# A delta-rule attention and gated layer on one core: the state product as one 64-column tile, the solve on pairs of batch elements, results moved by ScalarE, and another written order

## The chip, the cores and the metric

The kernel runs on one core of one Trainium2 chip. The metric is the device time of one execution in microseconds, lower is better. TensorE (PE in the profile) multiplies matrices, VectorE (DVE), ScalarE (ACT) and GpSimd (POOL) work on elements, SyncE (SP) issues the transfers. All data are 32-bit floats.

## The reference

Two parts, the second fed by the first. For each of 4 batch elements (B) and 8 heads (H), over 768 tokens of 48 numbers:

```python
k_n = k / (norm(k) + 1e-6)
for t in range(S):                       # state is 48 x 48, zero at first
    y[t] = q[t] @ state
    v_old = k_n[t] @ state
    state = state + beta[t] * outer(k_n[t], v[t] - v_old)
```

Then, with x the 3072 x 384 matrix of all y (a row per batch element and token, all heads side by side):

```python
h = x @ w_in                             # 384 -> 2048
out = (h * cos(h)) @ w_out               # 2048 -> 384
```

## The kernel before

**Units.** The 768 tokens are cut into 24 units n of C = 32 tokens. In a unit the 4 batch elements lie in the four quarters of the 128 partitions, and the 8 heads are written as h = 2j + par, with j of 4 pairs and par of 2. The recurrence of a unit is solved in closed form: with the Gram matrix of its keys, the inverse of a 32 x 32 triangular matrix for each batch element and head gives all corrected values at once. Two units form a pair m, which shares one inverse.

**Steps of a unit**, as the tasks are called in the function that writes the program:

- `k`, `q`, `v` load; `square`, `sum`, `norms`, `scale`, `weigh` make the norms and the weights by beta. The root in `norms` is on GpSimd (L467).
- `turn`, `turn_out` transpose keys and queries: for n < 8 on TensorE with two copies by ScalarE (L525), later by `blocks` loads and one VectorE transpose (L531).
- `gram` (L546) multiplies keys with keys and queries; `gram_keys`, `gram_queries` scale the two results; `gram_put`, `gram_get` carry the Gram matrices through DRAM into the layout of the inverse.
- `inv` (L656, L663) is the inverse of pair m on GpSimd, in seven pieces of columns (pair 0 on VectorE, by halves); `put`, `get` carry it through DRAM back into `zt`.
- `state` (L713) multiplies keys and queries with the state of the units before. It runs over a (keys or queries), j, b and par: 64 matmuls, each with 32 weight columns and 48 moving columns, into the quarter of its batch element.
- `right` (L728, VectorE) subtracts the product with the keys, read from PSUM, from the values; `solve` (L776) multiplies with the inverse: 32 matmuls of 32 x 32 weights, one for each head and batch element; `solve_out` (L786) weighs the result.
- `update` (L799), `update_out` (L807) add to the state: 16 matmuls of 64 x 64 weights and 96 moving columns.
- `within` (L816) adds the part of the unit's own tokens to the product with the queries, in the same PSUM tile `p_kq`; `within_out` (L827, ScalarE, one copy of 128 x 384) takes it out; `features`, `features_out` (L835, L843) transpose it for the second part.

So the chain from unit to unit is state, right, solve, solve_out, update, update_out.

**The second part** works on one pair's 256 tokens p at a time: `hidden` (L856) or `layer` (L975) for the first product, `turns`, `rest`, `cos`, `gate` for h cos(h) on ScalarE and VectorE, `out` (L1001, L1058) for the second product. From p = 2 (first product) and p = 1 (second) on a scheme of seven products in place of eight is used, with sums by VectorE. The weights come as pairs of 32-bit words and are narrowed once at the start: `weights` (load), `split` (ScalarE), `shift` (VectorE), `add` (GpSimd, L438), 28 tiles, of which 0 to 11 are `w_in`.

**The order** is written out by hand. Each step is a task with an engine and the tasks it depends on; a list of numbers, `Order.LINE`, gives the place of every task in the program. Each engine takes its own tasks strictly in this order, and so does the transfer queue of SP. The costs that stand beside the tasks are not used when the program is written.

**Buffers.** `p_kq` and the tile for the smaller products (`two`) have one PSUM buffer each, the first product of the second part has three. `zt` has two buffers.

Of the kernel before, what the change touches and what calls it, by code (L numbers as in the profile page):

```python
# [53 lines left out]
0 1767 1 2 14 10 11 12 3 7 4 37 5 42 15 72 6 38 13 39 16 43 73 40 1768 1771 17 44 19 96 75 1769 97  # L54
79 18 1770 45 46 1775 80 76 48 47 77 20 99 104 1772 100 78 101 1779 1773 105 81 102 1774 49 82 106
50 83 84 1776 107 1783 108 9 131 51 22 52 109 1787 53 1780 36 1784 54 155 1781 55 56 132 1777 1788
41 1778 1791 111 1789 134 1782 110 1785 21 1790 138 8 1786 135 1795 23 139 136 186 818 1792 24
1793 112 25 137 1799 1796 26 57 27 113 1797 28 1803 74 29 30 1794 156 32 31 114 1807 140 33 210
141 142 34 58 115 35 1811 1808 98 189 59 1804 60 190 1798 679 61 1815 1800 116 103 133 1809 1805
1819 62 241 680 1812 1810 63 681 64 117 65 1820 66 1823 68 67 187 69 1821 159 682 118 265 1801 684  # L60
160 1816 1827 161 1817 685 86 162 1824 163 686 70 1822 119 87 71 143 1813 193 1802 243 1825 1818
689 1831 1828 683 164 1826 194 1829 85 687 1830 690 688 1806 719 1835 691 731 165 1814 732 1832
244 88 191 166 822 694 692 1833 1839 157 1836 89 1834 1837 90 695 92 1838 696 1843 699 693 697 167
91 93 1840 698 94 1841 700 704 1847 168 1844 701 211 192 95 702 709 703 1845 1848 1851 1842 120
733 705 714 1846 1849 710 158 1850 711 195 1855 169 712 121 196 197 198 706 720 713 707 122 715
1859 708 1856 170 716 747 1857 717 123 1863 1860 296 752 124 1852 245 718 748 749 125 753 1853
1858 127 750 126 757 1864 1854 1867 188 754 128 171 751 755 735 129 1865 758 762 130 759 1871 1868
320 756 760 1861 1866 214 763 736 767 1862 215 737 761 172 764 1869 765 772 1875 248 1872 766 768
1873 216 247 769 1874 145 246 1876 1870 777 217 773 1877 219 298 269 739 770 1878 740 721 774 173
771 775 743 778 220 299 722 212 779 744 780 745 782 249 723 221 300 724 776 788 174 725 783 268  # L70
784 222 741 785 726 218 819 823 824 144 223 825 727 820 821 302 146 786 728 224 781 303 213 147
729 734 175 148 787 225 149 789 151 791 351 790 150 152 738 153 793 792 176 154 226 794 177 270
242 178 796 179 795 227 180 798 182 375 181 799 183 301 184 800 185 228 826 827 250 828 742 730
829 324 251 252 801 831 830 353 253 833 842 271 832 843 266 200 834 844 835 272 229 845 802 274
836 354 804 273 355 201 323 837 839 838 806 846 797 275 807 276 847 850 199 808 267 848 840 809
230 851 849 852 810 841 277 803 854 202 853 858 855 304 860 859 278 856 203 357 862 857 204 863
805 206 890 358 279 811 207 861 205 873 864 812 406 231 874 865 875 814 232 280 233 866 234 813
868 867 876 297 235 746 281 869 237 236 815 430 877 878 208 870 325 209 238 879 816 282 239 881
871 880 240 378 882 921 872 920 889 922 885 321 283 892 883 886 408 305 884 379 895 255 887 306
409 923 307 308 891 356 925 410 888 896 926 893 284 326 817 894 898 327 924 329 328 927 936 900  # L80
897 929 322 901 254 930 928 902 411 330 331 931 256 285 933 903 937 932 938 904 940 939 906 941
332 257 942 908 934 944 943 258 333 909 935 905 910 948 945 949 259 946 261 950 334 461 947 952
911 984 954 953 951 262 260 956 359 912 335 957 899 958 413 955 286 907 967 959 960 412 287 336
968 962 961 380 913 969 352 963 288 914 971 964 289 337 970 290 972 292 485 291 973 916 975 263
976 917 338 974 977 965 293 918 264 978 376 987 294 983 295 966 1014 915 1015 979 433 1017 1016
980 463 981 1019 339 1018 434 360 982 1030 310 361 1020 985 1021 1031 363 362 1023 1032 464 986
1024 1022 309 465 1033 381 989 1025 382 383 384 990 988 1026 992 311 1034 340 1027 994 991 919 414
312 1038 385 995 386 467 1039 1035 996 1040 313 1036 1028 997 993 387 1037 314 1029 316 516 315
1042 998 317 1043 388 1046 466 1044 318 341 319 1041 1047 1078 1000 342 468 377 389 1048 1045 407
1050 1049 1001 1052 1051 1002 343 1053 390 1054 344 1056 1055 431 345 1057 347 346 1003 348 540  # L90
391 435 1065 1061 1004 1066 349 1067 1005 1058 1062 999 1068 1006 392 488 1069 1007 1063 1070 1059
1064 1071 1008 350 393 1009 1010 1072 489 1081 1109 1060 1011 1108 1073 1110 1111 1012 518 1074
519 1113 1075 1077 1112 520 432 1124 1080 1013 1114 394 1125 415 1076 1126 365 416 1083 417 418
1115 469 1084 366 523 1116 1086 1082 1127 1117 1079 364 436 1118 1088 1119 437 438 439 1089 1087
1120 1090 1128 367 1129 1121 368 1130 440 441 1085 369 1132 395 1131 371 1133 1122 372 1091 571
1134 1092 1123 442 370 1136 1094 1135 1137 1140 1172 396 522 1141 443 1096 1138 1095 1142 397 1093
462 1139 1144 1143 444 398 1145 1146 1155 1148 1147 399 1097 1149 486 1156 1150 445 1157 1098 1151
1159 400 1099 402 595 401 1100 521 446 373 1158 1152 374 490 403 404 1160 1101 544 1161 1153 447
405 1162 1163 1102 470 1154 1103 420 1164 1167 471 573 1203 1168 473 448 1165 1104 472 1202 1169
491 1204 1170 1105 1166 492 1205 493 494 1106 421 1207 1206 1209 524 1218 449 1171 1208 1219 1174  # L100
1175 495 1210 1211 1177 1173 1213 574 1212 419 1220 1178 1214 575 1221 1180 1222 1107 496 543 1223
1215 1179 497 1224 1176 1216 1226 1225 578 1227 1234 1182 498 1228 1217 422 450 1183 1230 423 1181
577 1184 1229 499 424 1185 1231 426 626 1186 427 1232 1235 1188 1187 425 500 1236 1233 1238 1237
1190 1240 1239 1249 451 1241 501 1250 1242 452 1251 1244 545 517 1243 453 1245 1191 1252 1253 502
454 1192 455 1193 1254 457 650 456 1194 1255 503 1256 428 1246 429 487 458 1189 459 1195 460 576
541 1257 1247 1196 1258 1197 598 525 628 1296 475 1259 1248 1198 526 504 1261 527 599 1260 1199
1269 546 1200 1297 528 547 548 1265 1262 1266 549 1263 1268 1267 1264 1299 1271 505 579 1298 629
1301 1201 1303 1300 1302 630 550 1272 1312 1304 474 1270 1305 476 1307 1313 1306 633 551 1274 1308
1314 631 552 1309 632 1315 1276 477 1320 1277 478 553 1273 1278 1321 479 1275 1322 1279 481 1316
1323 1310 554 482 1317 480 1318 1280 1311 1319 1282 1324 555 506 1325 1328 507 1283 1330 572 1329  # L110
1284 1326 600 1332 556 1327 508 1333 1331 1334 509 1343 1336 1281 596 510 1344 512 557 511 1345
654 1285 1337 1335 542 483 1338 484 653 1286 1339 558 1346 1347 1340 513 1348 514 1287 1351 1341
1360 1349 1352 515 1288 1353 1390 1289 1354 580 1290 559 1350 530 1291 581 1342 1292 583 582 1355
1293 1356 1363 601 1357 1294 1391 602 1393 1358 1392 604 634 1395 1394 560 1359 1396 1406 1362
1407 605 606 1397 531 1365 1295 1408 1399 1398 529 1361 1366 1400 603 1409 1401 1368 1402 607 1410
1403 1370 1364 1367 532 1414 1411 608 1404 1412 1415 533 1416 1371 1417 1372 1413 609 1405 1422
597 1418 1424 1423 1419 1373 534 1420 1425 610 536 535 1374 537 1437 1376 1438 1375 561 1439 611
1440 1426 1378 1428 562 1427 1377 1379 627 655 563 1429 612 1380 564 1430 1369 1454 565 1431 651
567 566 1432 613 538 1433 1434 568 1421 539 1441 1381 569 1445 1382 1442 1446 1383 1443 1447 1435
1384 570 1444 1448 614 1485 1385 1436 1487 1486 1449 635 1450 585 636 1451 1488 638 1386 1484 1500  # L120
1387 637 584 1457 656 1388 1489 657 658 659 1453 586 1490 1501 1456 1452 1502 1491 1459 1503 587
1455 1493 1492 660 588 1495 1494 615 1460 1496 1458 1389 1462 1504 661 1505 589 662 591 1506 590
1497 1507 1464 1498 1508 663 1509 1516 1499 1510 1465 1463 1512 1511 1517 1466 664 1518 1467 1513
1514 1520 1519 1468 1515 1521 665 592 1548 1522 1531 1470 1523 1532 1524 1472 1533 1469 1526 1525
# [53 lines left out]
def kernel(  # L178
# [502 lines left out]
    def get(n):  # L681
# [13 lines left out]
        for b in range(B):  # L695
            queue("get", n).dma_start(out=zts[n][quarter(b)], in_=z_dr[b])
# [845 lines left out]
```

## Time and profile before

| | us |
|---|---|
| median of 3 runs | 670.01 |
| lowest and highest | 668.9, 674.3 |
| span of the profiled execution | 670.2 |
| busy in it: TensorE | 616.5 |
| VectorE, ScalarE, GpSimd | 466.5, 242.4, 347.1 |
| TensorE's mean granted clock | 0.995 |

The profiled execution has no time of its own beside its span, from its first instruction to its last; the span is within 0.1% of the median of the runs. Busy times overlap across engines, so the largest share does not by itself say what sets the end. The state product's records sum to 33.5 us over 23 units, the solve's to 19.7 us over 22, the update's to 21.8 us over 23.

### The profile page before, as it was taken

The numbers are of one execution on the slowest core, as the hardware profiler recorded it, in microseconds if no ns is written. First come the engines' busy times: TensorE is split into PE (matmuls) and PEld (weight loads), VectorE is DVE, ScalarE is ACT, GpSimd is POOL, SyncE is SP. The second block draws the span as 40 slices with busy tenths as digits, with TensorE's granted clock in tenths as the row PEclk, the third lists the DMA queues.
The fourth block names the chain that finished last, engine by engine and source line by source line (L and its number), as shares of the span: only waits on it lengthen the run. The fifth ranks groups of instructions, "written<-read, shape, count | busy, mean of one in ns | idle before, by whom it ended". The sixth has DMA issues, their size and how long they took to land.

```text
span 670.2 us, 27723 instructions
## 1 busy us (share of the span) xinstructions
PE 616.5 (92%) x12120; PEld 580.5 (87%) x12120; DVE 466.5 (70%) x892; ACT 242.4 (36%) x416; POOL 347.1 (52%) x734
## 2 busy tenths in 40 slices
PE   4326789999999999999999999999999999999996
PEld 3225779976889999999999999999999999999996
DVE  6872698897577777787767767777776666656662
ACT  3441565650223433334334332333323333332420
POOL 4268778988728658238458484385383382000000
PEclk9999899999899999999999999999999999999999
DMA  8776594464364523544443624623312302000000
GB/s 179 183 177 156 130 228 124 105 110 66 53 103 68 85 54 57 89 88 70 70 83 55 108 35 73 106 39 53 69 27 39 68 2 40 20 2 24 1 25 24
DMA packets 215645, 51.80 MB, mean 77 GB/s; under 512 B 207076, under 2 KB 210420, under 8 KB 215524
## 3 DMA queue, kind: packets, MB, share of 16 engines
q1 hardware_dynamic: 212516, 49.16, 38.0%
q8 instruction: 95, 1.56, 1.0%
q10 hardware_dynamic: 2752, 0.43, 0.4%
q0 software_dynamic: 256, 0.44, 0.2%
q14 instruction: 26, 0.21, 0.1%
HBM read 39.24 MB, written 10.75 MB: 75 GB/s over the span
## 4 chain that ended last, share of the span: by engine, by line
PE 79%; DMA 7%; SPq 4%; POOL 4%; DVE 2%; issue 2%; ACT 0%; ACTq 0%; DVEq 0%; POOLq 0%
PE p_h L975 28%; PE p_out L1058 27%; PE p_h L856 5%; PE p_kq L713 4%; PE p_out L1001 3%; PE p_u L776 3%; PE p_s L799 3%; PE p_kq L816 2%; PE p_g L546 2%; POOL z L663 2%; DMA pairs<-in_moe_w_in_dram 2%; POOL part L656 2%; PE p_o L1058 2%; DMA qp<-in_q_dram 1%; SPq L310 1%
## 5 line engine op out<-in xcount | busy, mean ns | idle before, releaser
L656 POOL TENSOR_TENSOR part<-z,gb 128x126 f32<-128x126 f32 (+22 forms) x341 | 134.6, 395 | 116.1 <-DMA gb<-g_dr 75.0
L663 POOL TENSOR_TENSOR z<-z,part 128x126 f32<-128x126 f32 (+22 forms) x341 | 138.7, 407 | 26.7
L975 PE MATMUL p_h<-x_ffn,w_in 128*128 128x128 f32 x1120 | 143.0, 277 | 0.0
L975 PEld LDWEIGHTS p_h<-x_ffn,w_in 128*128 128x128 f32 x1120 | 134.2, 192 | 1.5
L1058 PE MATMUL p_out<-w_out,g_ffn 128*128 128x192 f32 x672 | 121.8, 330 | 2.0 <-issue 2.0
L1058 PEld LDWEIGHTS p_out<-w_out,g_ffn 128*128 128x128 f32 x672 | 108.7, 191 | 3.3 <-issue 2.1
L896 ACT ACTIVATE turns<-p_h,quarter_turn 128x512 int32<-128x512 f32 x96 | 65.8, 688 | 105.6 <-DVE p_h L994 72.1
L912 ACT ACTIVATE turns<-turns,halfpi 128x512 f32<-128x512 f32 x96 | 68.7, 721 | 64.3 <-DVE turns L903 63.7
L1058 PE MATMUL p_out<-w_sum,g_ffn 128*128 128x192 f32 x496 | 88.7, 329 | 0.0
L903 DVE SCALAR_TENSOR_TENSOR turns<-p_h,turns 128x512 f32<-128x512 f32 x96 | 65.3, 683 | 22.0 <-ACT turns L896 22.0
L1058 PEld LDWEIGHTS p_out<-w_sum,g_ffn 128*128 128x128 f32 x496 | 79.7, 190 | 0.8
L991 ACT COPY g_ffn<-p_h 128x512 f32<-128x512 f32 x60 | 35.0, 584 | 108.8 <-PE p_h L975 108.7
L1074 DVE TENSOR_TENSOR g_ffn<-g_ffn 128x512 f32<-128x512 f32 x88 | 62.3, 715 | 10.0 <-PE p_out L1058 8.9
L915 DVE TENSOR_TENSOR g_ffn<-turns,p_h 128x512 f32<-128x512 f32 x96 | 64.6, 677 | 6.6 <-ACT turns L912 6.5
L994 DVE TENSOR_TENSOR p_h<-g_ffn,p_h 128x512 f32<-128x512 f32 x60 | 41.5, 692 | 30.5 <-PE p_h L975 23.7
L467 POOL TENSOR_TENSOR knrm<-ksum,halves 128x16 f32<-128x16 f32 (+1 forms) x14 | 36.2, 2590 | 41.5 <-DVE ksum L455 41.5
L1108 DVE SCALAR_TENSOR_TENSOR o<-p_out,o 128x192 f32<-128x192 f32 x74 | 25.2, 353 | 35.4 <-PE p_out L1058 33.9
L856 PE MATMUL p_h<-x_ffn,w_in 128*128 128x128 f32 x384 | 47.3, 282 | 2.3 <-POOL part L656 2.1
L856 PEld LDWEIGHTS p_h<-x_ffn,w_in 128*128 128x128 f32 x384 | 45.8, 197 | 3.3 <-issue 2.2
L975 PE MATMUL p_h<-x_sum,in_sum 128*128 128x128 f32 x320 | 41.6, 277 | 0.0
L786 DVE TENSOR_TENSOR u<-p_u,bz 128x384 f32<-128x384 f32 x48 | 24.4, 550 | 21.9 <-PE p_u L776 21.8
L975 PEld LDWEIGHTS p_h<-x_sum,in_sum 128*128 128x128 f32 x320 | 38.7, 192 | 0.5
(110 smaller groups left out, 767.2 us busy)
## 6 DMA issues: line engine op xcount, KB each, us to landing
pairs<-in_moe_w_in_dram SPq DMA_DIRECT2D x12, 512.0 KB
pairs<-in_moe_w_out_dram SPq DMA_DIRECT2D x16, 384.0 KB
gb<-g_dr SPq DMA_DIRECT2D x22, 256.0 KB
vp<-in_v_dram SPq DMA_DIRECT2D x96, 48.0 KB
out_dram<-o SPq DMA_DIRECT2D x23, 192.0 KB
kp<-in_k_dram SPq DMA_DIRECT2D x128, 24.0 KB
z_dr<-z SPq DMA_DIRECT2D x11, 256.0 KB
zt<-z_dr SPq DMA_DIRECT2D x88, 32.0 KB
```

What stands on the lines that cost most here:

```text
L467: nc.gpsimd.tensor_tensor(out=scales[m][2][:, part], in0=sums[m, part.start][:, 0:n], in1=halves[:, 0:n], op=ALU.pow,)
L656: eng.tensor_tensor(out=part, in0=z[:, 0:rows, j, None].to_broadcast(shape), in1=a[:, j, None, j + 1 :].to_broadcast(shape), op=ALU.mult,)
L663: eng.tensor_tensor(out=behind, in0=behind, in1=part, op=ALU.subtract)
L856: nc.tensor.matmul(p_h[:, i], w_in[:, t, (4 * k + i) * 128 : (4 * k + i + 1) * 128], xts[p][:, t, unit * 128 : (unit + 1) * 128], start=(t ...
L896: nc.scalar.activation(turns[p, f], hidden_of(p, f), AF.Identity, bias=quarter_turn, scale=TURN)
L903: nc.vector.scalar_tensor_tensor(out=r, in0=hidden_of(p, f), scalar=TURN, in1=t, op0=ALU.mult, op1=ALU.subtract,)
L912: nc.scalar.activation(r, r, AF.Sin, bias=halfpi, scale=2.0 * math.pi)
L915: nc.vector.tensor_tensor(out=place(p, f), in0=step_of(rests.pop((p, f)), f), in1=step_of(hidden_of(p, f), f), op=ALU.mult,)
L975: nc.tensor.matmul(p_h[:, e], in_sum[:, odd_tile, 4 * s + e] if a == "s" else w_in[:, a, f * 128 : (f + 1) * 128], x_sums[p][:, unit] if b ...
L994: nc.vector.tensor_tensor(out=block(p, s, 0, 1) if i == 3 else p_h, in0=block(p, s, *one), in1=p_h, op=ALU.add,)
L1058: nc.tensor.matmul(p_o, left(p, part, a)[:, e % 4], right(e, b), start=(e == 0), stop=(e == FT // 2 - 1), skip_group_check=True,)
L1074: nc.vector.tensor_tensor(out=left(p, s, to), in0=left(p, s, one), in1=left(p, s, two), op=op)
```

## The change

1. **State product.** Transposed keys and queries of one batch element and head pair lie side by side: `kq_t` changes from (side, batch and pair, token) to (batch and pair, side, token). In odd batch elements the queries come first. One matmul takes all 64 columns as weights: 32 matmuls for 64. For batch elements 2i and 2i + 1 the result is a half of the partitions; the product with the keys of batch element b stands in quarter b, as before, that with its queries in quarter b xor 1.
2. **Moves.** `turn_out` for n < 8 is four ScalarE copies in place of two, `turn_blocks` three VectorE transposes in place of one, of as many elements in all. The loads of `blocks` write another place, with as many transfers of the same size.
3. **Old values.** A new task `old` (L735 of the new kernel) copies the product with the keys from PSUM into `rhs` by ScalarE, four copies of 32 partitions; `right` then subtracts SBUF from SBUF.
4. **Solve.** Two lasting tiles `zt_pairs`, zeroed once by GpSimd, hold the inverses of batch elements 2i and 2i + 1 as diagonal blocks of 64 x 64. For n > 1 the solve is 16 matmuls for 32. For n < 8 both parities write the half they read from, from n = 8 on the odd parity writes the other half. `get(n)` now depends on `solve(n - 2)`.
5. **Output.** `within` writes into quarter b xor 1, and `within_out` is four copies of 32 partitions.
6. `part` and `fold` share one lasting tile.

```diff
     def turn_out(n):
         kq_t = turned(n)
         p_t = p_ts.pop(n)
         for a in range(2):
-            nc.scalar.copy(
-                kq_t[:, a].rearrange("p (b j) t -> p j b t", b=B),
-                p_t[:, a].rearrange("p j (b t) -> p j b t", b=B),
-            )
+            for x in range(2):
+                nc.scalar.copy(
+                    sides(kq_t, x)[:, a ^ x].rearrange("p b j t -> p j b t"),
+                    p_t[:, a].rearrange("p j (b x t) -> p x j b t", x=2, t=C)[:, x],
+                )
...
-                        kq_t[rows48(par), 0, b * NP + j],
-                        kq_t[rows48(par), :, b * NP + j],
+                        kq_t[rows48(par), b * NP + j, b % 2],
+                        kq_t[rows48(par), b * NP + j, :: 1 - b % 2 * 2],
...
-        zts[n] = work.tile([128, H, C], FP, name="zt")
+        zts[n] = zt_pairs[n % 2]
...
-            queue("get", n).dma_start(out=zts[n][quarter(b)], in_=z_dr[b])
+            queue("get", n).dma_start(
+                out=zts[n][quarter(b), :, b % 2], in_=z_dr[b]
+            )
...
-        for a in range(2):
+        for x in range(2):
             for j in range(NP):
-                for b in range(B):
+                for i in range(2):
                     for par in range(2):
                         nc.tensor.matmul(
-                            p_kq[quarter(b), par, a, j],
-                            kq_t[rows48(par), a, b * NP + j],
-                            st[rows48(par), b // 2, j, b % 2],
-                            start=(j == 0 and a == 0),
-                            stop=(a == 0),
+                            p_kq[half(i), par, x, j],
+                            kq_t[rows48(par), (2 * i + x) * NP + j].rearrange("p s t -> p (s t)"),
+                            st[rows48(par), i, j, x],
+                            start=(j == 0 and x == 0),
+                            stop=True,
                             skip_group_check=True,
                         )
+
+    def old_values(n):
+        rhs = rhss[n] = work.tile([128, H, D], FP, name="rhs", bufs=1)
+        for b in range(B):
+            nc.scalar.copy(by_parity(rhs[quarter(b)]), p_kqs[n][quarter(b), :, b % 2])
...
-        rhs = rhss[n] = work.tile([128, H, D], FP, name="rhs", bufs=1)
-        nc.vector.tensor_tensor(
-            out=by_parity(rhs),
-            in0=by_parity(vt),
-            in1=p_kqs[n][:, :, 0],
-            op=ALU.subtract,
-        )
+        nc.vector.tensor_tensor(out=rhss[n], in0=vt, in1=rhss[n], op=ALU.subtract)
...
-                for b in range(B):
-                    h = 2 * j + par
-                    nc.tensor.matmul(
-                        p_u[home(n, b, par), par, j], zt[quarter(b), h], rhs[quarter(b), h]
-                    )
+                h = 2 * j + par
...
+                for i in range(2):
+                    to = half(1 - i if n >= PLAIN_TURNS and par else i)
+                    nc.tensor.matmul(p_u[to, par, j], zt[half(i), h], rhs[half(i), h])
...
-        nc.scalar.copy(by_parity(y), p_kqs.pop(n)[:, :, 1])
+        p_kq = p_kqs.pop(n)
+        for b in range(B):
+            nc.scalar.copy(by_parity(y[quarter(b)]), p_kq[quarter(b ^ 1), :, b % 2])
```

7. **The order.** `Order.LINE` is new as a whole. Read back into tasks, these are the stretches that the text below speaks of. (`inv1,0` is the first piece of inverse 1; numbers after a task are its unit, tile or pair.)

```
GpSimd before: norms0,0 norms0,1 add0 norms1,0 norms1,1 add1 add2 add3 add5 add4 norms2 inv1,0 inv1,1
               add6 inv1,2 inv1,3 add7 inv1,4 add10 inv1,5 inv1,6 add13 add8 add12 add14 add15 add9 add11
GpSimd after:  norms0,0 norms0,1 norms1,0 norms1,1 add1 add2 inv1,0 add0 norms2 inv1,1 inv1,2 add5 add3
               inv1,3 add4 inv1,4 add7 add6 inv1,5 inv1,6 add10 add8 add12 add9 add11 add13 add15 add14
SP before, from gram_put3:  gram_put3 weights5 v1 k5 put0 q4 weights6 gram_get1 get0 ... v4 weights13 k8
               weights14 q6 k9 weights15 put1 gram_put4 weights16 gram_put5 get2
SP after:      gram_put3 v0 weights5 k4 gram_get1 v1 put0 k5 weights6 get0 ... k8 weights12 q5 weights13
               v3 weights14 put1 q6 weights15 gram_put5 get2
SP before, after solve5:  k13 store0,1 blocks11,1 gram_put8 v9 put3 gram_put9 blocks11,0 gram_get4 get6
SP after, after solve5:   blocks11,1 blocks10,0 store0,1 v8 gram_put9 put3 gram_put8 gram_get4 get6
TensorE before: state1 solve_half1 hidden0,0 between1 solve1 update1 within1 turn5 hidden0,2 gram5 state2
TensorE after:  state1 features0 hidden0,0 solve_half1 hidden0,2 between1 solve1 update1 turn5 within1 gram5 state2
TensorE after, unit 5: within4 out1,0,1 state5 features4 out1,1,0 solve5 ... within5 out1,2,0 features5
```

In the new order TensorE has long stretches of other work between state product and solve in the even units from 4 on, and little in the odd ones: `features` and a half `out` in unit 5, `layer` 5 and 6 in unit 7, `layer` 3 and 4 and a half `out` in unit 9, two halves of `out` in unit 13, and two to six such pieces in the others.

## The prediction

> **What bounds the kernel now.** I read the page first: the shares, the slices and the chain.
>
> ```profile
> PE 616.5 (92%) x12120; PEld 580.5 (87%) x12120; DVE 466.5 (70%) x892; ACT 242.4 (36%) x416; POOL 347.1 (52%) x734
> PE   4326789999999999999999999999999999999996
> PE 79%; DMA 7%; SPq 4%; POOL 4%; DVE 2%; issue 2%; ACT 0%; ACTq 0%; DVEq 0%; POOLq 0%
> ```
>
> TensorE is the bound from the seventh slice on (a slice is 16.8 us) and not before. The table by stretches (stretch; its length; busy us of PE, weight loads, DVE, ACT, POOL; granted clock; DMA) gives both parts their size, and the list of TensorE's waits from 100 us on (us, times, longest) what is left there:
>
> ```profile
> 40.00:60.00 20.00, 11.28 (x394) 9.49 (x395) 11.48 (x23) 4.77 (x9) 16.43 (x30) 1.00 0.66 163
> 60.00:80.00 20.00, 13.29 (x430) 12.34 (x414) 9.77 (x15) 8.42 (x16) 14.94 (x32) 0.91 0.71 173
> 80.00:100.00 20.00, 18.29 (x455) 16.01 (x454) 17.41 (x30) 12.76 (x25) 16.14 (x20) 1.00 0.85 198
> 100.00:670.20 570.20, 560.19 (x10573) 531.88 (x10571) 397.35 (x732) 199.79 (x339) 283.67 (x637) 1.00 0.33 60
> ```
>
> ```profile
> PE p_u L776 <- DMA zt<-z_dr: 2.6, 2, 1.6
> PE p_out L1058 <- issue: 2.0, 1, 2.0
> ```
>
> After 100 us TensorE is busy for 560.2 of 570.2 us, and 5 of the rest are the last stores. A microsecond taken off TensorE there is a microsecond of span, and so is one added. Between 40 and 100 us it idles for 17 us: the second place where the change can act.
>
> Then TensorE's timeline, for what a small product costs (start, duration, line, shapes, passes; each fp32 matmul is two passes):
>
> ```profile
> 397.40 1.38 PE L713 MATMUL p_kq<-st,kq_t 48*32 48x48 f32 x128
> 398.70 2.05 PE L975 MATMUL p_h<-x_ffn,w_in 128*128 128x128 f32 x16
> 400.69 0.80 PE L776 MATMUL p_u<-rhs,zt 32*32 32x48 f32 x64
> 401.42 2.87 PE L1058 MATMUL p_out<-w_sum,g_ffn 128*128 128x192 f32 x16
> 404.22 0.89 PE L799 MATMUL p_s<-u,kp 64*64 64x96 f32 x32
> 405.04 0.80 PE L816 MATMUL p_kq<-u,tt 32*32 32x48 f32 x64
> ...
> 462.91 0.80 PE L546 MATMUL p_g<-kq_t 48*32 48x64 f32 x60
> 463.56 1.61 PE L713 MATMUL p_kq<-st,kq_t 48*32 48x48 f32 x127
> ```
>
> The cost is start to next start: the state product 1.31 us for 64 matmuls, the solve 0.73 (0.81 for units below 8, by the same reading), the update 0.82. The state product's passes follow each other at 8.35 ns, so 128 passes are 1.07 us and 0.24 is filling and draining.
>
> **State product on 64 columns.** 32 matmuls take the place of 64, on four tiles of 64x64 with 48 moving columns. No such group exists here; the nearest is the update, with the same tiles and 96 moving columns. In its records four passes start together, the next four 0.133 us later, then a round of four every 0.0825 us, and the next group 0.193 us after the last round's start: 0.133 + 6 x 0.0825 + 0.193 = 0.82. The round is its moving columns: 192 columns at full array pass in 162 ns, 384 in 322, so 0.83 ns a column, and 96 x 0.83 + 2.5 = 82.5. The new round loads the same 64 weight columns, so it cannot be longer than 82.5 ns; with 48 moving columns it cannot be shorter than 42.5. Between these: 16 full-array passes of L975 take 1.78 us, 111 ns each, and each loads 128 new weight columns while the pass before it streams; 64 columns then need up to 56 ns. I take 56 ns: the load sets the round. 16 rounds are 0.133 + 14 x 0.056 + 0.153 = 1.07 us (the tail is 40 ns shorter); the bounds give 0.88 and 1.44. For units 4 to 23: 20 x (1.07 - 1.31) = -4.8 us (-8.6 to +2.6).
>
> The Trainium skill, page "TensorE: Matmul & The Clock Gate", section "Part 3: Packing small matmuls — row/col tiling", speaks against this: a weight load overlaps running matmuls only when it goes to another row group. By that rule load and stream would add up; the trace disagrees, since the update's round of 82.5 ns has no room for a load behind its stream.
>
> Lost with it: gram and state product now share a tile shape, and where one follows the other the gram goes by in 0.58 us (462.91 to the first state pass at 463.49) in place of 0.79. With another shape behind it each pays 0.79: nine such pairs from unit 4 on, +1.9 us.
>
> **Solve on pairs.** 16 matmuls for 32. From unit 8 on all four tiles are used: 8 rounds, 0.133 + 6 x 0.056 + 0.153 = 0.62 against 0.73, 16 x -0.11 = -1.8 (bounds -3.0 to +0.8). For units 2 to 7 both parities go to the same two tiles, two passes a round, 16 rounds, 1.07 against 0.81: +1.6 (+0.4 to +3.8). Together -0.2.
>
> **Results by ScalarE.** No row has a copy of 32 partitions; the nearest are
>
> ```profile
> L827 ACT COPY y<-p_kq 128x384 f32<-128x384 f32 x24 | 11.5, 478 | 41.7 <-PE p_kq L816 39.1 <-PE p_z L835 2.4
> L525 ACT COPY kq_t<-p_t 128x512 f32<-128x512 f32 x16 | 8.6, 586 | 7.0 <-PE p_t L515 6.9
> ```
>
> A copy with another behind it follows at 0.10 us less. If only the 384 elements a partition count, four copies last 3 x 0.38 + 0.48 = 1.62 us; if the partitions counted in full, 0.48 in all. I take 1.62. ScalarE gains 23 x (1.62 + 1.14) = 63 us, 36% becomes 46%, and TensorE waited for none of its results after 100 us: as throughput it costs nothing. As latency: state, copies, subtraction, solve is now 0.05 + 1.62 + 0.06 + 0.55 + 0.1 = 2.4 us instead of about 0.7. TensorE's work between state and solve covers it in even units (11 to 24 us). In odd units the new order leaves, at 1.31 us for a half `out` of 8 passes, 0.89 for 8 passes of `layer` and 0.33 for `features`, 1.64 (unit 5), 2.67 (7), 3.1 (9), 6 (11), 2.6 (13), 4.4, 4.0, 3.5, 4.0 and 5.3 us. Unit 5 stalls for 0.8; its state product waits 0.4 for the output copies of unit 4 (1.7 against one product of 1.31), its features 0.4 likewise. Units 7, 9, 13 and 19, with one ScalarE or VectorE step ahead, 0.7 together. Sum +2.3 (0 if the copies cost by partitions).
>
> The subtraction now reads SBUF twice. In the trace such an operation is mostly steady (L503 0.96 us) but was 1.91 at 36.1 us, while GpSimd worked; L728, with an operand in PSUM, stayed within 0.52 to 0.56. The Trainium skill, page "SBUF — State Buffer", section "Who interferes with whom", has the rule: two SBUF inputs contend with a GpSimd instruction that reads SBUF. By it a subtraction would wait up to one inverse step, here 0.5 us; the 0.7 above has room for that.
>
> The three transposes in place of one (16 units, about +0.3 us each) lie on VectorE at 70%. The two memsets lie in GpSimd's 4.5 idle us before 9.1 us; uncovered, at most 1.28 each. The gets wait for the solve two units earlier, as two buffers did before.
>
> **The new order at the start.** Solve(2) stood at 92.4 us behind this:
>
> ```profile
> 44.64 3.28 POOL L467 TENSOR_TENSOR knrm<-ksum,halves 128x16 f32<-128x16 f32 x1 [1.22 <-DVE ksum L455]
> 47.89 0.23 POOL L656 TENSOR_TENSOR part<-z,gb 128x31 f32<-128x31 f32 x1
> 71.57 1.67 POOL L438 TENSOR_TENSOR w_in<-w_in,pairs 128x512 uint32<-128x512 uint32 x1 [2.94 <-DVE w_in L434]
> ```
>
> Inverse 1 starts behind the root of pair 2 and waits 2.94 us for a weight tile; its put goes out at 83.1. In the new order its fetch stands before the second v load and put(0), so its data are there near 36; the first piece goes ahead of that root, and the tile waited for goes behind the inverse. From 36 us GpSimd has 28.0 us of inverse, 3.3 of root, 6 adds of 1.3 and some 1.5 of waiting for the root's sum: 36 + 28 + 3.3 + 7.8 + 1.5 = 76.6, 6 us earlier. On SP, k(9), q(6) and v(4) (8 us) now stand behind that put; q(6) is the tight one, since turn(6) asks for it near 82 us, the others serve steps not due for 40 us. TensorE can use it: hidden(0,2) now fills the time in which solve_half(1) and between(1) left gaps of 0.7, 2.07 and 2.59 us, and the granted clock of 0.91 between 60 and 80 us costs more. The weights set a limit (hidden(0,4) needs an add near 80), so I take 4 of the 6: -4 (-7 to +2).
>
> Later, get(6) had k(13), v(9) and half of blocks(11) ahead of it on SP, 10 us of issue, and now only v(8), 1.9: the 1.6 us wait for zt goes, -1.5.
>
> **Sum:** -4.8 + 1.9 - 0.2 + 2.3 - 4 - 1.5 = -6.3 on the profiled span of 670.2, which is the median of the runs (670.0) within 0.1%: 664 us.
>
> **Rivals.**
> 1. The start is given back: weights and VectorE (87% busy from 80 to 100 us) hold TensorE where they did. For: SP issues almost without pause until 100 us. Against: the sum on GpSimd. 668 us.
> 2. The round runs at its moving columns, 42.5 ns: state 0.88, solves 0.54 and 0.88; 3.8 + 2.4 less, 658 us. For: loads on four tiles run at once in the update. Against: 111 ns for a full load.
> 3. Slower: ScalarE's queue. Its order is fixed; a cosine ahead of the copies waits for VectorE (63.7 us over 45 waits, 1.4 on the mean, 5.3 the longest), and the copies behind it hold the solve. With 2.8 us of delay (one wait, two operations) the odd units stall by 3.6 + 2.5 + 2.1 + 2.6 + 0.8 + 1.2 + 1.7 + 1.2 = 15.7, less the 1.5 counted: 678 us. From a delay of 1.8 us on the gain is gone. Against: in units 7, 13 and 17 the copies come first after the state product.
> 4. Load and stream add up, 96 ns a round: state 1.63, solves 0.86 and 1.63; 20 x 0.56 + 16 x 0.24 + 6 x 0.56 = 18 more, 682 us. It is what the rule of the Trainium skill on row groups would make of it. Against: the update.
>
> **Chances.** Forecast 0.47, rivals 0.19, 0.13, 0.17 and 0.04. A measurement of this kernel (runs from 668.9 to 674.3) tells about 1%, 6.7 us, from no change. The forecast lies at that edge: 0.27 faster, 0.18 same, 0.02 slower; rival 1 0.17 same, 0.02 slower; rival 2 faster; rival 3 0.15 slower, 0.02 same; rival 4 slower. Faster 0.40, same 0.37, slower 0.23. The range, 656 to 678, holds rivals 1 to 3; the forecast's own is 658 to 670.
>
> **What would show it.** State groups near 1.07 us start to next start (0.88: rival 2; 1.4 or more: wrong), solves 0.62 and 1.07; the put of inverse 1 near 77 us and solve(2) near 87; ACT copies of 0.48 us; TensorE's waits from 100 us on at 5 to 7 us, unit 5 the largest. Waits for rhs over 8 us mean rival 3; a solve(2) at 92 us means rival 1.

## The result, and the profile after

The changed kernel takes 677.74 us (median of 19 runs, 675.86 to 681.23). The kernel before, run beside it, takes 673.36 (668.9 to 677.35); its first three runs had given 670.0. The ratio is 1.0079, with a 95% interval of 1.0059 to 1.0099: slower by 0.8%, where 664 was forecast. The profiled execution of the changed kernel spans 677.6 us, that of before 670.2, so the profiles show 7.4 us of difference and can be compared stretch by stretch. That is 3 us more than the medians show; each profile is one execution, and what the stretches say may be off by as much.

The page of the changed kernel: busy times, TensorE by slices, and its granted clock by slices.

```profile
PE 614.0 (91%) x9944; PEld 575.3 (85%) x9944; DVE 459.9 (68%) x924; ACT 319.5 (47%) x596; POOL 349.3 (52%) x736
PE   3316759999999999999999999999999999999996
PEclk9999869999999998999999999999999999999999
```

TensorE issues 9944 passes for 12120, as the change has it, and ScalarE is busy at 47% (forecast 46%). But the sixth slice (about 85 to 102 us) is new: TensorE is half idle there and its granted clock falls. The table by stretches of the changed kernel, with the columns of the prediction's table:

```profile
40.00:60.00 20.00, 7.04 (x226) 5.76 (x225) 5.64 (x12) 6.94 (x14) 13.30 (x27) 1.00 0.59 132
60.00:80.00 20.00, 15.13 (x446) 13.47 (x439) 12.17 (x17) 11.10 (x21) 18.37 (x28) 0.83 0.48 120
80.00:100.00 20.00, 10.36 (x248) 9.31 (x249) 8.71 (x16) 7.62 (x17) 12.59 (x21) 0.66 0.44 97
100.00:677.60 577.60, 567.46 (x8743) 535.50 (x8742) 407.74 (x787) 279.18 (x509) 291.39 (x643) 1.00 0.35 65
```

Against before, TensorE does 4.2 us less from 40 to 60 us and 7.9 us less from 80 to 100, and the other engines are idler there too, except ScalarE from 40 to 60 us. From 100 us on, 10.1 us are not TensorE's; before it was 10.0. The milestone that tells the two halves apart is the start of solve(2), from the timelines of TensorE, before and after:

```profile
92.37 0.88 PE L776 MATMUL p_u<-rhs,zt 32*32 32x48 f32 x64
...
104.92 1.14 PE L795 MATMUL p_u<-rhs,zt 64*64 64x48 f32 x32
```

So the start lost 12.5 us, and all that follows takes 572.7 us in place of 577.8, a gain of 5.1.

What the steady part looks like, in the timeline of TensorE (start, duration, line, shapes, passes; L726 is the state product, L557 the Gram product, L795 the solve):

```profile
412.56 0.68 PE L795 MATMUL p_u<-rhs,zt 64*64 64x48 f32 x32
413.17 1.05 PE L994 MATMUL p_h<-x_ffn,w_in 128*128 128x128 f32 x7
...
423.96 0.86 PE L557 MATMUL p_g<-kq_t 48*32 48x64 f32 x64
424.75 1.15 PE L726 MATMUL p_kq<-st,kq_t 48*64 48x48 f32 x64
425.82 2.38 PE L1077 MATMUL p_out<-w_out,g_ffn 128*128 128x192 f32 x13
```

Start to next start the state product takes 1.08 us in nearly all units from 3 on (1.11 once), and the solve 0.61 in most from 8 on.

What the start looks like, in the timeline of the changed kernel (the bracket is the engine's idle time before, and what ended it; L420 loads a weight tile, L443 is `add` on GpSimd, L428 `split` on ScalarE, L534 the copies of `turn_out`, L688 the put):

```profile
40.42 0.24 POOL L667 TENSOR_TENSOR part<-z,gb 128x31 f32<-128x31 f32 x1 [10.63 <-DMA vp<-in_v_dram]
...
86.10 2.51 POOL L443 TENSOR_TENSOR w_in<-w_in,pairs 128x512 uint32<-128x512 uint32 x2
87.40 0.35 SPq L420 DMA_DIRECT2D pairs<-in_moe_w_out_dram  x1
...
90.24 0.43 SPq L688 DMA_DIRECT2D z_dr<-z  x1
90.55 0.55 ACT L428 ACTIVATE w_out<-pairs 128x384 f32<-128x384 f32 x1 [11.85 <-DMA pairs<-in_moe_w_out_dram]
...
92.04 1.17 ACT L534 COPY kq_t<-p_t 128x256 f32<-128x256 f32 x4
...
93.26 1.19 PE L557 MATMUL p_g<-kq_t 48*32 48x64 f32 x64 [7.42 <-ACT kq_t L534]
```

Read from below: gram(5) on TensorE waits 7.42 us for the copies of turn(5). These stand on ScalarE behind split(13), which has waited 11.85 us for weight tile 13. Its load went out at 87.40, when the first of the adds that begin at 86.10 had ended: add(10), which frees one of the eight buffers that weight tiles pass through. In the new order add(10) stands on GpSimd behind the last pieces of inverse 1; before it stood ahead of them. Nothing needs tile 13 before the products of `w_out`, near 110 us; it is only that the copies queue behind it. The put of inverse 1 queues too: the inverse ended at 86.1, but on SP its put stood behind this load and the next one and went out at 90.24. (The bracket of the first line names a load of v, but inverse 1 reads the fetched Gram matrix, issued at 34.7, and a start value that ScalarE had copied by 37.4.)

### The profile page after: what moved, and what is told of

It reads as the page before. It is cut to its first block, busy times and chain, and to the rows that moved or that the text cites. A ratio compares the mean times of both kernels' runs of the same rounds, so it can differ in the third digit from the quotient of the medians.

```text
span 677.6 us, 23595 instructions
## 1 busy us (share of the span) xinstructions
PE 614.0 (91%) x9944; PEld 575.3 (85%) x9944; DVE 459.9 (68%) x924; ACT 319.5 (47%) x596; POOL 349.3 (52%) x736
## 4 chain that ended last, share of the span: by engine, by line
PE 80%; DMA 7%; POOL 4%; DVE 3%; ACT 3%; SPq 1%; issue 1%; ACTq 0%; POOLq 0%; DVEq 0%
PE p_h L994 28%; PE p_out L1077 27%; PE p_h L875 5%; PE p_kq L726 3%; PE p_out L1020 3%; PE p_s L816 3%; PE p_u L795 2%; PE p_kq L833 2%; PE p_g L557 2%; PE p_o L1077 2%; DMA kp<-in_k_dram 1%; POOL part L667 1%; PE p_z L854 1%; DMA halves_z<-z_dr 1%; POOL w_in L443 1%; POOL z L674 1%
## 5 line engine op out<-in xcount | busy, mean ns | idle before, releaser
L674 POOL TENSOR_TENSOR z<-z,part 128x126 f32<-128x126 f32 (+22 forms) x341 | 142.9, 419 | 26.7
L1077 PE MATMUL p_out<-w_sum,g_ffn 128*128 128x192 f32 x496 | 90.8, 331 | 0.0
L846 ACT COPY y<-p_kq 32x384 f32<-32x384 f32 x96 | 45.1, 469 | 30.9 <-PE p_kq L833 24.0
L738 ACT COPY rhs<-p_kq 32x384 f32<-32x384 f32 x92 | 43.0, 468 | 9.2 <-PE p_kq L726 8.3
L472 POOL TENSOR_TENSOR knrm<-ksum,halves 128x16 f32<-128x16 f32 (+1 forms) x14 | 35.9, 2564 | 10.3 <-DVE ksum L460 10.3
```

The lines of the kernel that those rows point to most:

```text
L674: eng.tensor_tensor(out=behind, in0=behind, in1=part, op=ALU.subtract)
L738: nc.scalar.copy(by_parity(rhs[quarter(b)]), p_kqs[n][quarter(b), :, b % 2])
L846: nc.scalar.copy(by_parity(y[quarter(b)]), p_kq[quarter(b ^ 1), :, b % 2])
L1077: nc.tensor.matmul(p_o, left(p, part, a)[:, e % 4], right(e, b), start=(e == 0), stop=(e == FT // 2 - 1), skip_group_check=True,)
```

## Experiments

Each ratio is to the kernel before, run beside it. TensorE's time without work from 100 us to the end (about 5 us of it the last stores) is read from the table by stretches. Places at the start are read from one profile of each kernel. The runs with add(10) moved and with the splits moved have the same program as the changed kernel up to inverse 1, and it begins at 39.0 and 39.3 us there and at 40.4 here; so a difference of up to 1.4 us at the start tells nothing.

**The start, one cause at a time.** add(10) back ahead of inverse 1's last pieces:

```diff
 GpSimd
-inv1,4 add7 add6 inv1,5 inv1,6 add10 add8
+inv1,4 add7 add6 add10 inv1,5 inv1,6 add8
```

> The changed kernel, with one move on GpSimd: add(10) stands ahead of the last two pieces of inverse 1, as it did in the old order, in place of behind them. Theory (the queue at the start): add(10) frees the buffer for which the load of weight tile 13 waits on SP, split(13) on ScalarE waits for that load, and the copies of turn(5) stand behind split(13). Then the load goes out near 77 us (87.4 in the changed kernel), the third product gram(5) starts near 86.5 (93.3), solve(2) near 98.5 (104.9), and the time is 6 us below the changed kernel: 671.5. Rival 1 (inverse 1 itself sets the start): it ends 1.3 us later, near 87.4, and solve(2) waits for zt in place of gram(5) for its copies: solve(2) 103 or later, 676 or more. Rival 2 (the loss lies in the ScalarE copies of the odd units): no change, 677.5.

672.14 us, ratio 1.0001 (0.9976 to 1.0026): 5.6 us below the changed kernel. Tile 13 is loaded at 75.4, gram(5) starts at 85.3, solve(2) begins at 95.2 and goes on at 97.0 after a short wait for zt. The first theory holds; the wait of rival 1 is there, but it is 1.4 us.

The same block seen from ScalarE: add(10) and the load stay late, only the splits move, and with them the steps of VectorE and GpSimd that follow them.

```diff
 ScalarE
-turns0,2 split12 split13 cos0,2 turn_out5 within_out1 cos0,0 old2 features_out1
+turns0,2 cos0,2 turn_out5 within_out1 cos0,0 old2 split12 split13 features_out1
```

> The changed kernel, with add(10) left behind inverse 1 and weight tile 13 as late as there, but split(12) and split(13), with the steps of VectorE and GpSimd that follow them, moved behind old(2) on ScalarE. It takes away only what stood behind the late load on ScalarE's queue. Theory (the copies of turn(5) stood behind a split that nothing needs yet): the load still goes out near 87 us, but gram(5) starts near 86.5 (93.3), solve(2) near 98.5, 671.5, as with add(10) moved. Rival (the late weight tiles themselves hold TensorE): gram(5) may be early, but the products wait for tiles and the time stays at 676 or above.

675.21 us, ratio 1.0054 (1.0022 to 1.0085). gram(5) starts at 85.6 although tile 13 is still loaded late (85.4), so what held it was its place behind split(13), and not the weights. But solve(2) starts at 98.2 to 99.5, since put(1), still behind that load on SP, goes out only at 88.2, and the time lies between theory and rival, nearer the rival: a part of the gain is given back to the late inverse.

The other cause lies 40 us earlier: k(5) stood behind put(0) on SP, square(2) on ScalarE waited for it, and ScalarE's half of the fetch of inverse 0 stood behind square(2).

```diff
 SP
-gram_get1 v1 put0 k5 weights6 get0
+gram_get1 k5 put0 v1 weights6 get0
```

> The changed kernel, with k(5) and v(1) exchanged on SP: k(5) is loaded ahead of put(0), v(1) behind it. Theory: square(2) on ScalarE gets its data near 41 in place of 44 us, so ScalarE's half of the fetch of inverse 0, which stands behind it, goes out near 42 (44.0), solve_half(0) starts near 49 (51.3), add(5) on GpSimd waits about 1.5 us less (3.7), inverse 1 ends near 83.5 (86.1), and all that hangs on add(10) behind it moves with it: gram(5) near 90.7 (93.3), 675. Rival (the fetch is bound by the transfers that share the queues, not by its place): solve_half(0) stays at 51 and the time at 677.5.

675.36 us, ratio 1.0039 (1.0017 to 1.0060). solve_half(0) has its first data at 46.1 and goes on at 46.9 (48.3 and 51.3 in the changed kernel; 49.9 and 50.0 for the latter in the two profiles of the same program), earlier than expected; inverse 1 ends near 82.7, gram(5) starts at 90.1 and solve(2) at 101.7. The theory holds, by these places more than by the 2.4 us, for the two intervals just touch.

> Both moves together: add(10) ahead of the last two pieces of inverse 1, and k(5) ahead of put(0) with v(1) behind it. Theory (two causes in one queue of waits): solve_half(0) near 49, weight tile 13 loaded near 75, gram(5) near 84.5, solve(2) near 96.5, 669. If the two share one cause, no more than the better of the two alone, 671.5 or above. If the start is not the loss: 677.

669.67 us, ratio 0.9943 (0.9920 to 0.9967): the changed code with both moves is faster than either kernel. The timeline of this kernel at the place that was 7.42 us late, and at solve(2):

```profile
83.55 1.19 PE L557 MATMUL p_g<-kq_t 48*32 48x64 f32 x64 [0.46 <-ACT kq_t L534]
...
95.72 1.13 PE L795 MATMUL p_u<-rhs,zt 64*64 64x48 f32 x32
```

Two moves of single tasks bring solve(2) from 104.9 to 95.7; the rest of the run takes 571.9 us, as in the changed kernel (572.7).

**Code and order apart.** First the new code in the old order:

```diff
 every engine: the old order
-state(n) right(n)
+state(n) old(n) right(n)
```

> The code of the changed kernel in the old order of the kernel before; each copy of old values stands right behind its state product. It tells code from order. Theory (the start is lost by the order, and the new products are as fast as predicted): solve_half(0) near 46 and solve(2) near 92.5, as before; state products 1.08 us and solves 0.61 start to next start. In the old order the odd units have less work between state product and solve: 1.3 us in units 5, 7 and 21, 1.8 in 13, 15, 22 and 23, where the copies need about 2.4, so stalls of 1.1 three times and 0.6 four times, 5.7 in all, against the gain of 3.1: 670 + 2.6 = 673, between 670 and 677. Rival (the code brings the loss to the start: copies on ScalarE, the zero tiles on GpSimd): solve(2) near 98 or later, and 677 or more.

693.88 us, ratio 1.0310 (1.0267 to 1.0353): far above the theory's 670 to 677; the rival's "677 or more" covers it, but names no cause for so much. solve(2) starts at 97.2, 4.8 late, near the rival's 98, so the code costs the start something of its own. And from 100 us on 28.9 us are not TensorE's, where it was 10.0. The list of TensorE's waits of this kernel from 100 us on (us, times, longest):

```profile
PE p_h L994 <- DVE g_ffn L934: 4.5, 3, 2.4
PE p_z L854 <- ACT y L846: 3.7, 6, 0.7
PE p_u L795 <- DVE rhs L745: 3.0, 3, 1.2
```

No single wait stands out; results of ScalarE and of VectorE are both late. So the new order does carry the new code: without it TensorE stands idle for 19 us more than before. Where they cost it, the next run asks:

```diff
-            nc.scalar.copy(by_parity(rhs[quarter(b)]), p_kqs[n][quarter(b), :, b % 2])
...
-        nc.vector.tensor_tensor(out=rhss[n], in0=vt, in1=rhss[n], op=ALU.subtract)
+        for b in range(B):
+            nc.vector.tensor_tensor(
+                out=by_parity(rhss[n][quarter(b)]), in0=by_parity(vt[quarter(b)]),
+                in1=p_kqs[n][quarter(b), :, b % 2], op=ALU.subtract,
+            )
```

> The new code in the old order, as in the run of the code alone (693.9), but without the copies of old values by ScalarE: VectorE subtracts the product with the keys straight from PSUM, in four instructions of 32 partitions. Theory (the 18 us that TensorE idles more in that run come from ScalarE's queue: copies that wait for a state product and hold what stands behind them, and one engine more in the chain to the solve): the chain from state product to solve is one handover shorter and ScalarE has 43 us less, so a half comes back: 684, between 680 and 688. Rival (it is VectorE that is late: 28 us more of work there): 692 or above.

685.84 us, ratio 1.0209 (1.0152 to 1.0266), 21.2 us without TensorE after 100 us: a good third of the loss goes with the copies of old values on ScalarE. solve(2) stays at 97.5, so these copies are not what the code costs the start. The same edit in the order with both moves:

> Both moves at the start, and VectorE subtracts the product with the keys straight from PSUM in four instructions of 32 partitions, without the copies of old values by ScalarE. In the old order this took 8 us off the new code (693.9 to 685.8). Theory (the new order gives the copies their cover, as the prediction's +2.3 us said): no more than 2 us are there to be had, less what 30 us more work on VectorE cost: 669, between 667.5 and 670.5. Rival (the copies cost the new order as they cost the old one): 662 to 665. Second rival (VectorE becomes late): 672 or above.

679.60 us, ratio 1.0125 (1.0082 to 1.0167): 10 us slower than with the copies (1.8% by the two ratios, taken in different sessions), the second rival. The largest of TensorE's waits in it from 100 us on:

```profile
PE p_u L797 <- DVE rhs L744: 2.8, 5, 0.8
```

VectorE is busy for 499 us (462 with both moves), and 19.0 us from 100 us on are not TensorE's (10.3). Waits for VectorE are half of what the list of this kernel adds up to. In the new order the old values are better on ScalarE than on VectorE.

Now the old code in the new order:

```diff
 every engine: the new order
-state(n) old(n) right(n)
+state(n) right(n)
```

> The code of the kernel before in the new order (without the steps for old values, which it does not have). It tells order from code from the other side. Theory (the loss at the start is the order's): weight tile 13 goes out near 86 us, gram(5) starts near 92, solve(2) near 104, as in the changed kernel; from there on the old products cost 5.4 us more in state products and 1.2 in solves and 1.8 less in Gram products and features: 677.6 + 4.8 = 682. Rival (the copies and the zero tiles delay the start): solve(2) near 95 and 673.

694.77 us, ratio 1.0342 (1.0292 to 1.0393). The start is as expected from the theory: gram(5) at 89.1 after a wait of 7.12 for its copies, solve(2) at 100.2. But the time is 12.8 us above the forecast, and all of that is lost later. The timeline of TensorE of this kernel shows where, in the middle of one state product (L711):

```profile
235.60 1.01 PE L711 MATMUL p_kq<-st,kq_t 48*32 48x48 f32 x88
239.02 0.78 PE L711 MATMUL p_kq<-st,kq_t 48*32 48x48 f32 x39 [2.42 <-issue]
```

After 89 of 128 passes TensorE stops for 2.42 us, and waits for nothing that the profile shows. There are nine such gaps from 0.4 us up after 100 us, 15.5 us in all; 9.2 of it is in state products, 7.1 in those next to a Gram product. The queue of TensorE's instructions in the transfers of the same kernel, from 236.6 to 237.7 us (packets, MB, share):

```profile
q8 instruction: 1, 0.02, 5.5%
```

A packet of 16 KB, began at 236.63 and took 0.96 (the one before began at 228.4, the next at 240.5); the gap ended 1.44 us after it. For all gaps of 1.5 us and more after 100 us it is 1.25 to 1.44. The queue carries 95 such packets here, one for every 256 of 24,240 matmuls and weight loads. The test moves six state products and a Gram product away from each other:

```diff
 TensorE, units 8, 10, 12, 14, 16, 18 (unit 8 shown)
-gram11 state8 layer3,0,2 out2,1,0 layer3,0,3
+gram11 layer3,0,2 out2,1,0 layer3,0,3 state8
 TensorE, unit 6
-state6 gram8 layer2,0,0 layer2,0,1
+state6 layer2,0,0 layer2,0,1 gram8
```

> The code of the kernel before in the new order, as in the run of the order alone (694.8), but the state products of units 8, 10, 12, 14, 16 and 18 stand three to five steps of TensorE further back, and gram(8) two, so that no Gram product and state product follow each other. Even units have 11 to 24 us between state product and solve, so this alone costs nothing. Theory (the gaps of 1.5 to 2.5 us inside state products of that run are TensorE waiting for its own code: each followed a 16 KB packet of its instruction queue by about 1.4 us, and two small products in a row use up 512 instructions in 2.1 us where packets of 256 came no closer than 3.3 us): the gaps inside state products, 9.6 us in all, go, and the time falls by 7 to 10 us, to 686. Rival (the gaps belong to the state products' operands or to the buffer, not to the code): they move along, 693 or above.

685.99 us, ratio 1.0217 (1.0172 to 1.0263), 8.8 us less with the same work. Of TensorE's waits from 100 us on, those without a releaser are now, among others,

```profile
PE p_g L544 <- issue: 1.9, 1, 1.9
...
PE p_kq L711 <- issue: 1.6, 2, 1.4
```

so those of the state products fell from 9.6 us (shorter gaps included) to 1.6; none is left in the moved ones. The theory holds in the main; 2.2 of the 9.6 stood in unit 13, which was not moved, and went as well.

**Trying for more at the start.** The prediction had inverse 1 begin near 36 us. Four runs fetched its data earlier, each with add(10) ahead of the last pieces as well.

```diff
 SP
-v0 weights5 k4 gram_get1 v1 put0 k5 weights6 get0
+v0 weights5 gram_get1 k4 k5 put0 get0 weights6 v1     (first)
+v0 weights5 gram_get1 v1 k4 put0 k5 get0 weights6     (second, third)
+v0 weights5 gram_get1 v1 put0 k4 get0 k5 weights6     (fourth)
 GpSimd
-inv1,0 add0 norms2 inv1,1
+inv1,0 add0 inv1,1 norms2
```

> Both moves, and three more at the start: the fetch of the Gram matrix of pair 1 ahead of k(4) on SP, the fetch of inverse 0 right behind its put (ahead of weight tile 6, v(1) and square(2)), and the root of pair 2 behind the second piece of inverse 1. Theory (the chain through inverse 0 and solve_half(0) still sets the start, and inverse 1 the weights behind it): inverse 1 starts near 38.5 (40.4), solve_half(0) near 44.5 (46.2 with both moves alone), GpSimd does not wait for the root's sum (1.8), inverse 1 ends near 80 (83.9), solve(2) near 93.5 (95.7), 667. Rival (the weights or TensorE itself hold the stretch from 60 to 95 us): 669.5, as with both moves alone.

673.46 us, ratio 1.0023 (0.9998 to 1.0048). v(0) and v(1) are both of pair 0: their weighing waited 11.1 us for v(1), until 50.1, and solve_half(0) started at 51.3.

> The changed kernel with add(10) ahead of the last two pieces of inverse 1, and another order at the start: on SP the fetch of the Gram matrix of pair 1, then v(1), k(4), put(0), k(5), the fetch of inverse 0; on ScalarE square(2) behind the fetch; the root of pair 2 behind the second piece of inverse 1. Unlike the earlier try (673.5), v(1) stays ahead: both v(0) and v(1) belong to pair 0, and solve_half(0) waited for v(1) there. Theory: solve_half(0) near 44.5 us (46.2 with the two moves alone), inverse 1 from 38 to 81 (40.4 to 83.9), solve(2) near 94 (95.7), 668. Rival (from 60 us on TensorE's own chain of small products at low clock and the weights hold the start, whatever comes earlier): 669.7.

672.92 us, ratio 1.0039 (1.0013 to 1.0065). Now ScalarE's copy of the start value of inverse 1 stood behind the fetch of inverse 0 until 44.5 us.

> As the run that started inverse 1 from an earlier fetch (672.9), with ScalarE's copy of the start value of inverse 1 ahead of the fetch of inverse 0, behind which it stood there until 44.5 us. Theory (the premise of the prediction: with its data there, inverse 1 starts early and everything at the start follows): inverse 1 from 38 us, without the wait for the root's sum, to about 80.5 (83.9 with the two moves alone), solve_half(0) near 46, solve(2) near 94, 668. Rival (TensorE's own chain of small products, at half pace after its idle times, holds the start by now): inverse 1 is early, solve(2) stays at 95.5 or later, 669.5 or more.

670.68 us, ratio 0.9972 (0.9944 to 1.0000). With the fetch issued at 32.5, 1.7 us earlier than with the two moves alone, inverse 1 begins at 39.4 (39.9 there) and ends at 85.6 (83.9); solve_half(0) starts at 47.6 (46.2) and solve(2) at 94.9 (95.7). By its time the rival is nearer, and its "inverse 1 is early" is not so either.

> The same, with put(0) ahead of k(4), the fetch of inverse 0 between k(4) and k(5). Theory (the chain from inverse 0 to solve_half(0) sets TensorE's start): put(0) goes out near 36 us (37.5), the fetch near 39.5 (42), solve_half(0) starts near 43.5 (46.2), solve(2) near 92.5 to 93.5, 666.5. Rival (the square of pair 2, now behind k(5) and the fetch, delays the root and with it gram(4), state(1) or inverse 1): solve(2) at 95 or later, 669.5 or more.

673.77 us, ratio 1.0013 (0.9995 to 1.0032). put(0) goes out at 35.9, but k(5) only at 44.4; square(2) and the copies of turn(4) behind it on ScalarE hold solve_half(0) until 50.6: the rival. The second of these orders with VectorE's subtraction:

> The order of the run just above with the subtraction of the other one (VectorE straight from PSUM). If both act and do not overlap, their differences to the two moves alone add up: 667. If the start is bound elsewhere, as the better of the two.

682.53 us, ratio 1.0178 (1.0121 to 1.0236), as far above the order with the copies as before (9.6 us). None of these beats the two moves.

## Why the prediction was wrong

The forecast was 664, the profile is 677.6. 13.7 us are missing, and one term has more than that: the start was put at -4 and is +12.5, 16.5 off. The rest came out 2.8 better than summed. By the medians, 4.4 us apart, the start would have lost nearer 9.5 than 12.5 if the rest gained the same 5.1; the sign of the term is wrong either way. That the time lies in the stated range, beside the 678 of rival 3, is chance: no rival had this cause.

- **State product, -4.8.** Right in its sum: 1.08 us for the 1.07 predicted. In the records the rounds of four follow each other at 58 ns for the 56 taken, the second comes 93 ns after the first for 133, and 168 ns follow the last for 153, so three small slips cancel. A round set by the load of 64 columns fits; no run changes the columns alone, so that it is the load is not shown. Over units 3 to 23 the groups sum to 22.7 us for 28.1, 0.6 more than forecast. Rivals 2 and 4, and with 4 the rule of the Trainium skill that it quotes, are out in this kernel.
- **Lost adjacency, +1.9.** Right: every Gram product after 100 us takes 0.79, where nine of those from unit 4 on took 0.58; Gram products and features together take 1.8 us more after 100 us.
- **Solve, -0.2.** Right: 0.61 and 1.06 for 0.62 and 1.07.
- **ScalarE's latency, +2.3.** Right in size, though four copies take 1.91 us, not 1.62: a copy of 32 partitions does not overlap the next (481 ns from start to start). The 1.6 counted around unit 5 came as the three waits for ScalarE below, 2.0 us in all; the 0.7 for units 7, 9, 13 and 19 did not come. The subtraction, now from SBUF twice, took 0.54 to 0.56 us in most units and at most 1.15, at 99.2 us while GpSimd worked. What TensorE waits for from 100 us on:

```profile
PE p_u L795 <- DMA zt<-z_dr: 1.3, 1, 1.3
PE p_t L520 <- DVE st L824: 1.0, 1, 1.0
PE p_u L795 <- ACT x_ffn L862: 0.9, 1, 0.9
PE p_z L854 <- ACT y L846: 0.6, 1, 0.6
PE p_kq L726 <- ACT y L846: 0.5, 1, 0.5
```

  Rival 3 did not happen; the waits in the old order show something like it.
- **zt, -1.5.** Right in size: 2.6 us of waits are 1.3. The 1.6 ahead of solve(6) went as forecast; that the 1.0 ahead of solve(16) went too, and 1.3 came up ahead of solve(8), was not foreseen.
- **Not in the sum.** The wait of 2.0 us in `out`, shown in the list before and passed over, looks like a wait for code: it ended 1.25 us after a packet of TensorE's instruction queue, as the gaps above did. In the changed kernel the longest of this kind after 100 us is 0.4. That is 1.5 of the 2.8.
- **The start, -4.** This step failed, in three places. It followed GpSimd's sum to the put of inverse 1 (put at 77, measured 90.2, of which 4.1 are its wait on SP behind the late loads) but not what the moved add releases: "the tile waited for goes behind the inverse" was costed as an add of 1.3 us, and its buffer, the load on SP, the split on ScalarE and the copies behind that were not followed. Moving it back is worth 5.6 us. It took k(9), q(6) and v(4) for what the put is moved past, but not k(5), which was moved behind put(0), with the square and ScalarE's half of the fetch behind it: 2.4 us alone, 8.1 with the other. And its sum was short: inverse 1 began at 40.4, not 36, since its data took 5.7 us from issue, and lasted 45.7 us, not 40.6: waits of 4.6 for 1.5 (0.9 for the root's sum, 3.7 for the data of add(5)), its pieces with what lies between them 29.9 for 28.0, adds 8.3 for 7.8, the root 2.9 for 3.3. Rival 1 had the right place, but only as a gain given back; a loss there was bounded at +2. A fourth part it put at nothing: the new code alone, in the old order, starts solve(2) 4.8 us late, and the old code in the new order 7.8 late (together 12.6; each is read from one profile). What in the code does that stays open.

The 3.3 us by which solve(2) is still late with both moves were not settled; they are less than the 4.8 that the code costs in the old order. Fetching earlier moved the start of inverse 1 by 0.5 us and solve(2) by 0.8, no more than profiles of one program differ. What the profile shows there is that products run slowly: in the run with both moves state(2) takes 1.89 us from start to next start for 1.08 later, at a granted clock of 0.74 between 80 and 100 us, where the kernel before had 1.00.

## What to carry to other kernels

When an order is written by hand, follow a moved step to what it releases, not only to what it computes: a buffer freed 12 us later stops a load, the load stops a queue, and the queue holds a step that has nothing to do with it. Price code and order as one thing: here each without the other costs 3%, and the pair, with two tasks put back, gains 0.6%. Before summing a gain in steady state, read the first idle stretch of the bound engine task by task; here it outweighed five terms that came out near their size.

## What the runs showed of the hardware

TensorE can run out of code. Its instructions come in packets of 16 KB for 256 of them, in none of the 16 profiles closer than 3.28 us from start to start, while the 128 passes of an old state product with their weight loads use up 256 in 1.07 us. In the old code with the new order five of nine pairs of a Gram and a state product after 100 us were stopped in the state product, for 0.3 to 2.5 us, and TensorE went on about 1.4 us after the packet. Two such products in a row need not stop it: in the kernel before none of ten pairs has a gap. Counting the instructions issued at each packet's start tells the difference. No packet set out while more than about 290 instructions were in stock (an estimate from all 16 profiles, by the instructions issued less 256 for each packet before: no packet set out before a count of 154 to 160, and TensorE never got past 449 without it). Where those 290 were used up in 1.3 to 2.6 us, in six places of the order run, TensorE stopped; in the kernel before the shortest such stretch after 100 us took 3.4. So it matters where in the count of 256 the pair falls. The page "Runtime: NRT & Kernel Launch" of the Trainium skill, section "Instruction fetch mechanics", has the blocks of 16 KB and 256 instructions, which the count of packets confirms, but calls the cost mostly hidden: in the order run with the old code it was 15.5 us. A side effect of the wider products is 78 packets for 95.

A ScalarE copy is not cheaper for having fewer partitions: those of 32 partitions and 384 elements take 469 ns on the mean, 478 with 128 partitions before.

```profile
L846 ACT COPY y<-p_kq 32x384 f32<-32x384 f32 x96 | 45.1, 469 | 30.9 <-PE p_kq L833 24.0 <-PE p_z L854 5.8
```
